# Thresholded attention and a gated feed-forward on one core: softmax turned in place in two tiles, PSUM banks of the product claimed early, operand remainders in place, and a new instruction order

## The chip, the cores and the metric

One Trainium2 chip, one of its cores. The metric is the device time of one execution in microseconds (us). Before the change it is 1448.93 us, the median of 3 runs (1448.88 to 1451.7).

## The reference, cut to what matters

Attention with 8 batches, 8 heads, 576 positions and heads of 64 in float32, then a feed-forward layer on the joined heads (512 wide, 1024 in the middle):

```python
scores = scale * np.matmul(q, k.transpose(0, 1, 3, 2))
thresh = np.max(scores, axis=-1, keepdims=True) - tau
scores = np.where(scores >= thresh, scores, -1000000000.0)
scores = scores - np.max(scores, axis=-1, keepdims=True)
attn = np.exp(scores)
attn = attn / (np.sum(attn, axis=-1, keepdims=True) + 1e-09)
x = np.matmul(attn, v)            # heads joined: batch, 576, 512
xk = mu_k * x + (1.0 - mu_k) * x_prev
xr = mu_r * x + (1.0 - mu_r) * x_prev
k = np.maximum(xk @ w_k, 0.0)
v = k * k @ w_v
r = 1.0 / (1.0 + np.exp(-(xr @ w_r)))
return r * v
```

x_prev is x moved by one position.

## The kernel before, in words

**Attention.** The unit of the attention is a *job*: one batch and one pair of heads. There are 36 of them (batch 0 is cut into two halves of 4 jobs each, batches 1 to 7 have 4 jobs each). A job has up to four units "P" of 128 query rows for both heads and a unit "T" for the last 64 rows of both heads together; a full job has the units 0, T, 1, 2, 3.

A unit goes through the engines like this. TensorE (PE) multiplies queries by keys into a PSUM tile `s` of two banks (L529, for T L503); there are two `s` tiles, so one for each head of a P unit. VectorE (DVE) takes the row maximum (L563); ScalarE (ACT) forms the threshold (L571) and the exponential into a tile `p` (L579); DVE zeroes what is below the threshold and sums (L587), then adds 1e-9 and inverts (L597, L598); GpSimd (POOL) multiplies `p` by the inverse (L612); DVE transposes 32x32 blocks of `p` into the job's tile `sq` (L630, for T L636). There are three `p` tiles and **one** `sq` tile. When all units of a job stand in `sq`, PE multiplies them by the values: 288 small matmuls (L666), here called the *product*, into four PSUM tiles `w` of one bank each; ACT copies these into `xT` and `xE` (L681, L688).

**Operands.** To keep float32 precision with the faster `fp32r` matmul, queries and keys are split: `hi` is the rounded value (ACT, L437), `lo` = `raw` - `hi` (POOL, L443). Eight DMAs of SyncE's queue (SP, L462) copy their halves into stacked tiles `st1`, `st2` (three buffers each, two used by a job); `raw` is scaled first (L419).

**Feed-forward.** When the four jobs of a batch (or half) are done, chunks of 256 positions follow, 18 in all: 16 "main" and two "end" chunks that gather the last 64 positions of four batches. A chunk has a difference (POOL, L753, tile `m`), four mixes (DVE, L762, tile `mk`), their splits (ACT L775, POOL L783), 96 matmuls for the first layer (L805), relu and square (ACT L813, L814) and split (L818, L828), 24 matmuls for the gate (L847), copy and sigmoid (ACT L851, L855), 48 matmuls for the last layer (L869), the final multiplication (DVE L875) and the store (L885). The three matmul groups take their PSUM tiles from the same tag `w` of four banks that the product uses; the product needs all four at once. The weights come as 64-bit words and are rebuilt at the start by DVE, ACT and POOL (L354 to L404).

**What sets the order.** The steps are not issued as they are written. Every step goes to `add` with an engine, a cost and a key; `Plan.order` places them one by one: of the steps that are ready it takes the one that can start first by the given costs, with ties to the lower key, and each engine then runs its instructions in that fixed order. A PSUM or SBUF buffer is given to whichever step is placed first (`loose` tags "w" and "r" in any order). Steps of the attention on PE have a key lowered by 1000; the first matmul of the product is placed only when `sq`, `v` and four `w` tiles are free for it at that moment.

Of the kernel before, what the change touches and what calls it, by code (L numbers as in the profile page):

```python
# [8 lines left out]
F32 = mybir.dt.float32  # L9
# [32 lines left out]
class Step:  # L42
    __slots__ = (
        "eng", "occ", "lat", "fn", "key", "deps", "succ", "allocs", "idx", "missing", "ready",
        "start", "end", "kb", "soft",
# [3 lines left out]
class Plan:  # L49
# [3 lines left out]
    HOP, LATE, FROM = 0.05, 0.3, 200.0  # L53
    SOFT = {"DVE": 0.3, "ACT": 0.3}
# [13 lines left out]
    def add(self, eng, occ, fn, reads=(), writes=(), key=0.0, lat=None, kb=0, wait=0.0):  # L68
        s = Step()
        s.soft = self.SOFT.get(eng, 0.0) if self.soft else 0.0  # L70
        s.eng, s.occ, s.fn, s.key, s.kb = eng, occ, fn, key, kb
# [40 lines left out]
    def order(self, loose=()):  # L112
# [27 lines left out]
        def when(s):  # L140
            t = s.ready
            hop = self.HOP
            if s.eng == "PE" and s.key < -500 and t > self.FROM:
                hop += self.LATE
# [15 lines left out]
        while len(out) < total:  # L160
# [38 lines left out]
            for j in s.succ:  # L199
# [3 lines left out]
                late = self.LATE if n.eng == "PE" and n.key < -500 and t > self.FROM else 0.0  # L203
# [14 lines left out]
def tile_threshold_attention_then_rwkv_ffn(  # L218
# [57 lines left out]
    def fixed(name, shape, dtype=F32):  # L276
# [3 lines left out]
    ident = fixed("ident", [P, P])  # L280
    add("POOL", 0.6, lambda: make_identity(nc, ident.get()), writes=[ident], key=-100)
# [9 lines left out]
        key=-100,  # L291
# [7 lines left out]
        key=-100,  # L299
# [7 lines left out]
        key=-100,  # L307
# [6 lines left out]
    for j in range(2):  # L314
        add("DVE", 0.1, lambda j=j: V.memset(xT[j].get()[:, :, 0:1], 0.0), writes=[(xT[j], "zero")], key=-99)
# [3 lines left out]
    bd = fixed("bd", [P, 2, P], FR)  # L319
    add("DVE", 0.3, lambda: V.memset(bd.get().bitcast(F32), 0.0), writes=[bd], key=-99)  # L320
# [9 lines left out]
    def weight(j, name, w, c, f, key, wait):  # L330
# [8 lines left out]
        def t():  # L339
# [9 lines left out]
            wait=wait,  # L349
# [7 lines left out]
            key=key,  # L357
# [3 lines left out]
            0.55,  # L361
            lambda: V.tensor_scalar(t(), t(), W_MIN, W_MAX, op0=ALU.max, op1=ALU.min),
            writes=box,
            key=key,
# [5 lines left out]
        def word(y):  # L370
# [4 lines left out]
            0.55,  # L375
            lambda: V.tensor_scalar(u(), u(), 0x07FFFFFF, 3, op0=ALU.bitwise_and, op1=ALU.logical_shift_left),
            writes=box,
            key=key,
# [3 lines left out]
            0.85,  # L382
# [5 lines left out]
            key=key,  # L388
# [3 lines left out]
            0.85,  # L392
# [5 lines left out]
            key=key,  # L398
        )
        add("ACT", 0.53, lambda: A.activation(piece.get()[:, 0], t(), AF.Copy), reads=box, writes=[(piece, 0)], key=key)  # L400
# [6 lines left out]
            key=key,  # L407
# [4 lines left out]
    def operands(job, key):  # L412
        b, hp = job["b"], job["hp"]
        raw = job["raw"] = sbuf("st1", [P, W], F32, 3) if job["plain"] else sbuf("raw", [P, W], F32, 1)
        add("DMA", DQ, lambda: SY.dma_start(raw.get(), qk[b, hp]), writes=[raw], key=key - PREP - 5, kb=576)
        add(
            "ACT",
            0.67,
            lambda: A.activation(raw.get()[:, 0:S], raw.get()[:, 0:S], AF.Copy, scale=small.get()[:, 2:3]),  # L419
            reads=[(small, 2)],  # L420
            writes=[raw],
            key=key - PREP,
        )
# [7 lines left out]
            kb=1152,  # L431
# [5 lines left out]
        add("ACT", 1.1, lambda: A.activation(hi.get(), raw.get(), AF.Copy), reads=[raw], writes=[hi], key=key - PREP)  # L437
        for y in range(2):
            cs = slice(0, S) if y == 0 else slice(S, W)
            add(  # L440
                "POOL",
                1.41 + 0.15 * y,
                lambda cs=cs: G.tensor_tensor(  # L443
                    lo.get()[:, cs], raw.get()[:, cs], hi.get()[:, cs].bitcast(F32), op=ALU.subtract
                ),
                reads=[raw, hi],
                writes=[(lo, y)],
                key=key - PREP,
            )
        job["st"] = [(sbuf("st1", [P, W], FR, 3), sbuf("st2", [P, S], FR, 3)) for _ in range(2)]  # L450
        for h in range(2):
            sl = slice(h * D, (h + 1) * D)
            t1, t2 = job["st"][h]

            up, dn = slice(0, D), slice(D, P)
# [526 lines left out]
```

## Time and profile before

| | |
|---|---|
| median of 3 runs | 1448.93 us |
| the profiled execution, its own time | 1451.04 us |
| its span in the profile | 1449.3 us |
| mean granted TensorE clock | 0.785 of full |
| busy: PE, DVE, ACT, POOL | 1017.6, 853.3, 643.5, 577.1 us |

The profile comes from one execution. "Busy" is time in which an engine ran at least one instruction. Since matmuls are pipelined, a busy PE is not a PE at its best rate. A row of the waits tells which engine sat idle before which line, and what ended the wait. A row of the stretches (windows) gives, for a time from A to B, its length, then for PE, PE's weight loads, DVE, ACT and POOL the busy us and the count of instructions, then the granted PE clock, the DMA share and GB/s.

### The profile page before, as it was taken

The page shows a single profiled execution, that of the slowest core. Times are in us where ns is not written, and L with a number is a line of the kernel's source. Part 1 is how long each engine was busy: PE and PEld are TensorE (multiplying, and loading weights), DVE is VectorE, ACT ScalarE, POOL GpSimd, SP SyncE. Part 2 cuts the span into 40 slices and gives each one's busy share as a digit, 9 for nine tenths or more (in the row PEclk, how much of TensorE's full clock was granted, in tenths as well). Part 3 has the DMA queues.
Part 4 walks back from the last instruction along what each step waited for, and adds up shares of the span by engine and source line. Part 5 has one row for each costly group of instructions (what it writes and reads, how often), then busy time and mean ns, then how long its engine had stood idle before and what let it go on. Part 6 is the DMA issues. An engine that isn't in the chain of part 4 may idle for free.

```text
span 1449.3 us, 34650 instructions
## 1 busy us (share of the span) xinstructions
PE 1017.6 (70%) x14608; PEld 903.6 (62%) x14608; DVE 853.3 (59%) x1657; ACT 643.5 (44%) x1447; POOL 577.1 (40%) x584
## 2 busy tenths in 40 slices
PE   3246748754995579655997568955797568955798
PEld 2236647544874478544996457854696457844687
DVE  5969648477707773477723768157753768167220
ACT  3437437243734355243743437334462437343342
POOL 3537436142713355142741337223461337222341
PEclk9558858767996579766998569975698569975799
DMA  9674644253304432254302335044422335042001
GB/s 283 193 241 124 179 140 107 73 140 115 91 27 137 114 101 56 73 140 115 91 23 69 103 100 140 23 118 121 124 57 73 102 100 136 30 116 59 2 15 30
DMA packets 41340, 147.81 MB, mean 102 GB/s; under 512 B 6880, under 2 KB 6880, under 8 KB 36576
## 3 DMA queue, kind: packets, MB, share of 16 engines
q1 hardware_dynamic: 41184, 145.59, 36.2%
q8 instruction: 116, 1.90, 0.5%
q14 instruction: 40, 0.33, 0.1%
HBM read 74.19 MB, written 9.44 MB: 58 GB/s over the span
## 4 chain that ended last, share of the span: by engine, by line
PE 60%; DVE 25%; issue 6%; DMA 5%; ACT 3%; SPq 1%; POOL 1%; DVEq 0%; POOLq 0%; ACTq 0%
PE w L666 15%; PE w L805 13%; PE w L869 13%; PE s L529 12%; DVE sq L630 7%; PE w L847 6%; DVE sm L563 6%; DVE p L587 5%; DVE mk L762 4%; DMA st<-lo 4%; ACT p L579 2%; DVE sq L636 1%; SPq L462 1%; PE s L503 1%; ACT sm L571 1%
## 5 line engine op out<-in xcount | busy, mean ns | idle before, releaser
L612 POOL TENSOR_SCALAR p<-p,sm 128x576 f32<-128x576 f32 x288 | 224.7, 792 | 537.6 <-DVE sm L598 531.8
L529 PE MATMUL s<-st 128*128 128x288 f32 x504 | 161.2, 413 | 266.8 <-DVE p L587 218.0
L666 PE MATMUL w<-sq,v 32*64 32x144 f32 (+2 forms) x10368 | 228.2, 337 | 128.7 <-issue 46.4
L666 PEld LDWEIGHTS w<-sq,v 32*64 32x64 f32 x10368 | 210.9, 170 | 149.3 <-issue 79.2
L529 PEld LDWEIGHTS s<-st 128*128 128x128 f32 x504 | 111.8, 265 | 301.5 <-issue 261.1
L630 DVE STREAM_TRANSPOSE sq<-p 128x1152 f32<-128x1152 f32 x128 | 175.4, 1370 | 181.8 <-PE w L666 172.8
L563 DVE TENSOR_REDUCE sm<-s 128x1 f32<-128x576 f32 x288 | 212.5, 750 | 89.3 <-PE s L529 79.7
L587 DVE SCALAR_TENSOR_TENSOR p<-s,sm,p 128x576 f32<-128x576 f32 x288 | 222.8, 800 | 11.0 <-ACT p L579 10.4
L805 PE MATMUL w<-xk,wk 128*128 128x256 f32 x1728 | 224.0, 288 | 4.6 <-ACT xk L775 2.4
L805 PEld LDWEIGHTS w<-xk,wk 128*128 128x128 f32 x1728 | 220.1, 196 | 6.5 <-ACT xk L775 2.8
L579 ACT ACTIVATE p<-s,sm 128x576 f32<-128x576 f32 x288 | 208.0, 725 | 0.1
L869 PE MATMUL w<-wv,k 128*128 128x512 f32 x864 | 200.6, 389 | 0.0
L571 ACT ACTIVATE sm<-sm,small 128x1 f32<-128x1 f32 x288 | 83.2, 291 | 261.1 <-DVE sm L563 257.0
L869 PEld LDWEIGHTS w<-wv,k 128*128 128x128 f32 x864 | 161.4, 188 | 32.6
L681 ACT ACTIVATE xT<-w 128x128 f32<-128x128 f32 (+1 forms) x144 | 34.4, 288 | 293.5 <-PE w L666 293.5
L875 DVE TENSOR_TENSOR sg<-w,sg 128x512 f32<-128x512 f32 x36 | 24.8, 690 | 223.5 <-PE w L869 204.1
L529 PE MATMUL s<-st,st 128*128 128x288 f32 x504 | 147.3, 385 | 0.0
L828 POOL TENSOR_TENSOR k<-r,k 128x512 fp32r<-128x512 f32 x72 | 93.5, 1300 | 94.1 <-ACT k L818 93.5
L762 DVE SCALAR_TENSOR_TENSOR mk<-m,mu_sb,xT 128x256 f32<-128x256 f32 x128 | 94.4, 778 | 42.0 <-POOL xk L783 32.0
L529 PEld LDWEIGHTS s<-st,st 128*128 128x128 f32 x504 | 116.9, 271 | 2.6 <-issue 2.5
L443 POOL TENSOR_TENSOR lo<-raw,hi 128x576 fp32r<-128x576 f32 x70 | 101.8, 1475 | 27.3 <-ACT hi L437 21.6
L783 POOL TENSOR_TENSOR xk<-mk,xk 128x512 fp32r<-128x512 f32 x72 | 92.4, 1283 | 50.1 <-ACT xk L775 49.8
(58 smaller groups left out, 934.5 us busy)
## 6 DMA issues: line engine op xcount, KB each, us to landing
v<-in_v SPq DMA_DIRECT2D x36, 1152.0 KB, 5.3
raw<-in_qk SPq DMA_DIRECT2D x35, 576.0 KB, 5.3
st<-hi SPq DMA_DIRECT2D x70, 288.0 KB, 3.1
st<-lo SPq DMA_DIRECT2D x70, 288.0 KB, 4.1
st<-hi SPq DMA_DIRECT2D x70, 144.0 KB, 3.4
st<-lo SPq DMA_DIRECT2D x70, 144.0 KB, 4.0
out<-sg SPq DMA_DIRECT2D x32, 256.0 KB, 2.0
wk<-in_w_k SPq DMA_DIRECT2D x8, 512.0 KB, 9.2
```

The costliest lines, as they stand in the source:

```text
L443: lambda cs=cs: G.tensor_tensor(lo.get()[:, cs], raw.get()[:, cs], hi.get()[:, cs].bitcast(F32), op=ALU.subtract),
L529: PE.matmul(ss[y].get()[:, z, 0:HS], l.get()[:, c * P : (c + 1) * P], r.get()[:, keys(z)], start=(j == 0), stop=(j == 1),)
L563: lambda sv=sv, col=col: V.tensor_reduce(col(0), sv(), axis=AX.XY, op=ALU.max, negate=True),
L571: lambda col=col: A.activation(col(1), col(0), AF.Identity, bias=small.get()[:, 1:2], scale=-1.0),
L579: lambda sv=sv, pv=pv, col=col: A.activation(pv(), sv(), AF.Exp, bias=col(0)),
L587: lambda sv=sv, pv=pv, col=col: V.scalar_tensor_tensor(pv(), sv(), col(1), pv(), op0=ALU.is_ge, op1=ALU.mult, accum_out=col(2)),
L612: lambda y=y: G.tensor_scalar(p.get()[:, y], p.get()[:, y], sm.get()[:, 3, y : y + 1], 0.0, op0=ALU.mult, op1=ALU.add),
L630: V.transpose(sq.get()[:, :, :, c * Q : (c + 1) * Q].rearrange("p b y i -> p y b i"), p.get().rearrange("p y (b i) -> p y b i", i=Q),)
L666: PE.matmul(os[a].get()[hs, 0:n], vt.get()[rows, j, hs], sq.get()[rows, j, h, lo:hi], start=(j == 0), stop=(j == NB - 1),)
L762: V.scalar_tensor_tensor(d.get()[:, y, o : o + n], diff.get()[:, y, o : o + n], mu_sb.get()[:, j, hc + y : hc + y + 1], prv[:, hc + y], op ...
L805: PE.matmul(h.get()[:, f], l, r, start=(ct == 0 and i == 0), stop=(ct == NCT - 1 and i == 2))
L869: PE.matmul(vps.get(), l, r, start=(ft == 0 and i == 0), stop=(ft == NFT - 1 and i == 2))
```

## The change

1. **Softmax in the job's tile.** The tiles `p` are gone. ACT's exponential writes straight into the job's `sq`, at the place where the unit's transposed blocks will stand; DVE's masking, POOL's scaling and DVE's transposition then all work in place there. `sq` has two buffers instead of one.
2. **The product's banks held ahead.** New PE steps without an instruction claim the four `w` tiles of the product (and the places in `xT`, `xE`) as soon as the last unit's inverse is computed, with the key -400; no chunk matmul can take them from then on.
3. **Remainders in place.** Queries and keys are loaded as two tiles instead of one `raw`; `lo` is written over the loaded tile. The copies into `st1`, `st2` become twelve DMAs of 144 KB instead of eight of 288 or 144 KB. For the T unit, `bd` is filled from `st1`, `st2` and its product has four steps of two matmuls instead of three.
4. **Chunk tiles.** `m` and `mk` are replaced by the two buffers of the tag `r`.
5. **The order.** Costs given to the planner are changed, a table `NUDGE` adds an offset to the key of each kind of step, and `LATE` and `SOFT` are smaller. The unused identity tile is gone.

The diff, cut to its core:

```diff
-    HOP, LATE, FROM = 0.05, 0.3, 200.0
-    SOFT = {"DVE": 0.3, "ACT": 0.3}
+    HOP, LATE, FROM, AHEAD = 0.05, 0.2, 200.0, 1000.0
+    SOFT = {"DVE": 0.15, "ACT": 0.15}
+    NUDGE = {
+        "act1": 6.0, "act10": -16.5, "act11": -27.5, "act12": -14.5, "act13": -6.0, "act14": -29.5, "act15": -3.0,
...
+        s.key = key + self.NUDGE.get(kind, 0.0)
...
-        hi, lo = job["hi"], job["lo"] = sbuf("hi", [P, W], FR), sbuf("lo", [P, W], FR)
...
+        for x, o in (("q", 0), ("k", S)):
+            raw = lo[x] = sbuf("lo" + x, [P, S], FR, LB[x])
+            top = hi[x] = sbuf("hi" + x, [P, S], FR, 1)
...
+                    raw.get(), raw.get().bitcast(F32), top.get().bitcast(F32), op=ALU.subtract
...
-            prods = [(0, hi), (0, lo), (1, hi)]
...
+            for h in range(2):
+                for v_ in range(2):
...
-        p = unit["p"] = sbuf("p", [P, 2, S], F32, PB)
+        sm = unit["sm"] = sbuf("sm", [P, 4, 2], F32, 4)
+        if job["sq"] is None:
+            job["sq"] = sbuf("sq", [P, NB, 2, NX], F32, 2)
...
+        def part(y):
+            if unit["kind"] == "P":
+                return sq.get()[:, :, y, c * Q : (c + 1) * Q]
+            return sq.get()[:, :, :, P:NX].rearrange("p b y i -> p (b y) i")
...
-            V.transpose(
-                sq.get()[:, :, :, c * Q : (c + 1) * Q].rearrange("p b y i -> p y b i"),
-                p.get().rearrange("p y (b i) -> p y b i", i=Q),
-            )
+            t = sq.get()[:, :, :, c * Q : (c + 1) * Q].rearrange("p b y i -> p (b y) i")
+            V.transpose(t, t)
...
+        last = job["units"][-1]
+        for o in os:
+            add("PE", 0.0, lambda: None, reads=[(last["sm"], (RES, 1))], writes=[o, *main, *tail], key=-400.0, lat=0.0, kind="pe4")
...
-            diff = sbuf("m", [P, 2, CH], F32, 1)
+            diff = sbuf("r", [P, 2, CH], F32, 2)
...
-                d = sbuf("mk", [P, 2, CH], F32, 1)
+                d = sbuf("r", [P, 2, CH], F32, 2)
```

How the order moves is shown at two places of the steady part of the program. First PE, around a job's product. Before, at the end of a batch (L869 is the last layer of a chunk, L666 the product; the last number in a tile's name tells one use from another):

```order
L869 MATMUL w_3_6187<-wv50_0_1485,k2_0_6058 128x512 x3
L869 MATMUL w_3_6187<-wv60_0_1684,k2_0_6058 128x512 x3
L869 MATMUL w_3_6187<-wv70_0_1689,k2_0_6058 128x512 x3
L666 MATMUL w_0_6216<-sq_0_5549,v_0_5547 64x144
L666 MATMUL w_1_6218<-sq_0_5549,v_0_5547 64x144
L666 MATMUL w_2_6220<-sq_0_5549,v_0_5547 64x144
L666 MATMUL w_3_6222<-sq_0_5549,v_0_5547 64x144
```

The changed kernel, one job's product (L843 is the first layer, L559 a score, L705 the product):

```order
L526 MATMUL s_1_7520<-st1_2_7118,bd_74 128x288 x4
L526 MATMUL s_1_7520<-st1_0_7394,bd_74 128x288 x4
L843 MATMUL w_2_7498<-xk_0_7214,wk31_0_623 128x256 x3
L843 MATMUL w_2_7498<-xk_0_7214,wk01_0_585 128x256 x3
L843 MATMUL w_2_7498<-xk_0_7214,wk11_0_601 128x256 x3
L843 MATMUL w_2_7498<-xk_0_7214,wk21_0_611 128x256 x3
L559 MATMUL s_0_7564<-st1_2_7118 128x288 x2
L559 MATMUL s_0_7564<-st1_2_7118,st2_1_7127 128x288 x2
L705 MATMUL w_3_7580<-sq_0_7057,v_0_7315 64x144
L705 MATMUL w_0_7582<-sq_0_7057,v_0_7315 64x144
```

Before, the product of a batch's last job stood behind the whole of two chunks, with no score matmul among the last 45 of L869, 96 of L805, 24 of L847 and 48 of L869. Now the product stands inside a chunk (its first layer goes on behind it) and scores of the next job stand just ahead of it. In the whole steady part of the new order one chunk lies spread over two jobs, and no more than 33 chunk matmuls stand between two scores. At the end of the program, after the last product, come 24 matmuls of L907 and then four whole chunks (96 of L843, 24 of L885, 48 of L907 each), where before there were three.

Second DVE, at the same two places. Before (L875 is the last step of a chunk, L630 and L636 transpose, L587 masks):

```order
L875 TENSOR_TENSOR sg_0_5899<-w_3_5972,sg_0_5899 128x512
L875 TENSOR_TENSOR sg_0_6149<-w_2_6160,sg_0_6149 128x512
L875 TENSOR_TENSOR sg_0_6149<-w_3_6187,sg_0_6149 128x512
L630 STREAM_TRANSPOSE sq_0_6366<-p_2_5768 128x2x18x32
L636 STREAM_TRANSPOSE sq_0_6366<-p_0_5847 128x36x16
L630 STREAM_TRANSPOSE sq_0_6366<-p_1_5888 128x2x18x32
L587 SCALAR_TENSOR_TENSOR p_2_6377,sm_0_5927<-s_0_5913,sm_0_5927,p_2_6377 128x576
```

And now (L605 maximum, L629 masks, L671 and L675 transpose, L639 and L640 invert):

```order
L605 TENSOR_REDUCE sm_1_7538<-s_1_7520 128x1
L629 SCALAR_TENSOR_TENSOR sq_1_7487,sm_2_7465<-s_0_7513,sm_2_7465,sq_1_7487 128x18x32
L671 STREAM_TRANSPOSE sq_0_7057<-sq_0_7057 128x36x32
L639 TENSOR_SCALAR sm_2_7465<-sm_2_7465 128x2
L640 RECIPROCAL sm_2_7465<-sm_2_7465 128x2
L629 SCALAR_TENSOR_TENSOR sq_1_7487,sm_1_7538<-s_1_7520,sm_1_7538,sq_1_7487 128x36x16
L605 TENSOR_REDUCE sm_3_7658<-s_0_7564 128x1
L639 TENSOR_SCALAR sm_1_7538<-sm_1_7538 128x1
L640 RECIPROCAL sm_1_7538<-sm_1_7538 128x1
L629 SCALAR_TENSOR_TENSOR sq_1_7487,sm_3_7658<-s_0_7564,sm_3_7658,sq_1_7487 128x18x32
L671 STREAM_TRANSPOSE sq_1_7487<-sq_1_7487 128x36x32
```

Before, the three transpositions into the next job's `sq` stood behind the chunks' last steps and needed the one `sq` that the product above (of `sq_0_5549`) still had to read. Now, behind the last transposition of a job (`sq_0_7057`), DVE has masks, a maximum and a transposition of the next job in the other tile (`sq_1_7487`) before it needs anything that PE makes after the product.

More of the change, by code (lines that the diff above doesn't have):

```diff
@@ L5 @@
 from concourse import mybir
-from concourse.masks import make_identity
 from concourse._compat import with_exitstack
@@ L348, in weight @@
             kb=512,
-            wait=wait,
+            wait=wait, kind="dma2",
         )
@@ L413, in operands, with scaled @@
         b, hp = job["b"], job["hp"]
[L414 to L422, printed above, removed]
-        )
+        def scaled(t):
+            add(
+                "ACT",
+                0.67,
+                lambda: A.activation(t()[:, 0:S], t()[:, 0:S], AF.Copy, scale=small.get()[:, 2:3]),
+                reads=[(small, 2)],
+                writes=[raw],
+                key=key - PREP, kind="act3",
+            )
+        if job["plain"]:
+            raw = job["raw"] = sbuf("st1", [P, W], F32, 3)
+            add("DMA", DQ, lambda: SY.dma_start(raw.get(), qk[b, hp]), writes=[raw], key=key - PREP - 5, kb=576, kind="dma3")
+            scaled(raw.get)
         vt = job["v"] = sbuf("v", [P, NB, P], F32, VB)
@@ L435, in operands @@
             return
-        hi, lo = job["hi"], job["lo"] = sbuf("hi", [P, W], FR), sbuf("lo", [P, W], FR)
-        add("ACT", 1.1, lambda: A.activation(hi.get(), raw.get(), AF.Copy), reads=[raw], writes=[hi], key=key - PREP)
-        for y in range(2):
-            cs = slice(0, S) if y == 0 else slice(S, W)
+        hi, lo = job["hi"], job["lo"] = {}, {}
+        st = job["st"] = [(sbuf("st1", [P, W], FR, 3), sbuf("st2", [P, S], FR, 3)) for _ in range(2)]
+        up, dn = slice(0, D), slice(D, P)
@@ new lines, in operands @@
+                lambda raw=raw, top=top: G.tensor_tensor(
+                    raw.get(), raw.get().bitcast(F32), top.get().bitcast(F32), op=ALU.subtract
+                ),
+                reads=[top],
+                writes=[raw],
+                key=key - PREP, kind="pool2",
+            )
+            for h in range(2):
+                sl = slice(h * D, (h + 1) * D)
+                moves = [(st[h][0], up, top), (st[h][0], dn, raw)]
+                if x == "q":
+                    moves += [(st[h][1], dn, top), (st[h][1], up, raw)]
+                for dst, rows, src in moves:
+                    fn = (lambda dst=dst, rows=rows, src=src, sl=sl, o=o: SY.dma_start(
+                        dst.get()[rows, o : o + S].bitcast(F32), src.get()[sl].bitcast(F32)
+                    ))
+                    add("DMA", DQ, fn, reads=[src], writes=[(dst, (rows.start, x))], key=key - PREP, kb=144, kind="dma6")
@@ L519, in both @@
                         )
-            add("PE", 3.0, both, reads=[raw], writes=list(ss.values()), key=key - 1000, lat=3.25)
+            add("PE", 3.0, both, reads=[raw], writes=list(ss.values()), key=key - 1000, lat=3.25, kind="pe2")
             return
@@ L769, in scale @@
                             )
-                add("DVE", 0.9 if nseg == 1 else 1.6, scale, reads=[diff, mu_sb, *sr], writes=[d], key=key)
+                add("DVE", 0.8 if nseg == 1 else 1.6, scale, reads=[diff, mu_sb, *sr], writes=[d], key=key, kind="dve14")
                 add(
```

227 lines of the change are left out of this document (114 added, 113 removed), and 6 rows, old and new, of the table NUDGE.

## The prediction

> **What bounds the kernel now.** I read the page first, then the stretches, the waits, the chain, and the timeline around one product. The page's first part gives no engine as the bound:
>
> ```profile
> PE 1017.6 (70%) x14608; PEld 903.6 (62%) x14608; DVE 853.3 (59%) x1657; ACT 643.5 (44%) x1447; POOL 577.1 (40%) x584
> ```
>
> No engine is busy over 70%, so the question is who waits for whom. The stretches tell it (from:to, length, busy us of PE, weight loads, DVE, ACT, POOL, granted clock):
>
> ```profile
> 0.00:210.00 210.00, 104.94 (x2624) 91.18 (x2624) 154.01 (x267) 97.30 (x214) 99.45 (x91) 0.73 0.67 195
> 453.00:473.00 20.00, 9.88 (x153) 8.83 (x138) 15.70 (x30) 9.81 (x27) 8.04 (x8) 0.67 0.63 171
> 518.00:550.00 32.00, 27.10 (x179) 25.53 (x177) 29.35 (x60) 25.48 (x59) 24.19 (x24) 0.89 0.58 153
> 534.00:550.00 16.00, 16.00 (x110) 14.86 (x108) 14.10 (x33) 14.89 (x31) 13.91 (x14) 1.00 0.45 104
> 561.00:589.00 28.00, 28.00 (x173) 24.86 (x173) 1.45 (x3) 9.71 (x15) 6.42 (x5) 1.00 0.06 20
> 943.00:1105.00 162.00, 119.00 (x1646) 106.59 (x1638) 96.27 (x188) 73.38 (x168) 63.72 (x65) 0.78 0.35 95
> ```
>
> 943:1105 is one whole batch: 4 jobs, 2 chunks, 162 us or 40.5 us a job, in which DVE works 96.27 us and PE 119.00. In 561:589, a whole chunk, PE works alone (DVE 1.45 of 28 us); in 453:473, attention alone, PE works half the time at 0.67 of its clock. Only in 518:550 do chunk and attention run side by side, and there DVE is busy 0.92 and PE 0.85 of the time. The two engines take turns, and the sum of the turns is the time. The waits of DVE show where its turns end (us in all, times, longest):
>
> ```profile
> DVE sg L875 <- PE w L869: 204.1, 24, 21.7
> DVE sq L630 <- PE w L666: 172.8, 30, 7.7
> DVE sm L563 <- PE s L529: 79.7, 150, 10.1
> ```
>
> 204.1 us DVE stands before a chunk's last step, which its fixed order puts ahead of the next softmax work; 172.8 us it stands before a transposition into `sq` until the product has read `sq`. The chain around one such place (start, us), then PE's and DVE's timeline there:
>
> ```profile
> 561.13 11.38 PE w L805 x96
> 572.51 5.50 PE w L847 x24
> 578.01 10.89 PE w L869 x48
> 588.93 0.70 DVE sg L875
> ```
> ```profile
> 588.82 0.47 PE L666 MATMUL w<-sq,v 32*64 32x144 f32 x6
> 589.68 4.21 PE L666 MATMUL w<-sq,v 32*64 32x144 f32 x254 [0.39 <-DVE sg L875]
> 595.03 0.74 PE L666 MATMUL w<-sq,v 32*64 32x144 f32 x28 [1.14 <-issue]
> ```
> ```profile
> 595.92 1.38 DVE L630 STREAM_TRANSPOSE sq<-p 128x1152 f32<-128x1152 f32 x1 [6.30 <-PE w L666]
> ```
>
> A chunk costs PE 11.38 + 5.50 + 10.89 = 27.77 us. The product waits behind it, since the chunk had the `w` tiles, then takes 595.77 - 588.82 = 6.95 us, and DVE waits 6.30 us of these.
>
> **The change part by part.**
>
> *Two `sq` tiles, banks held ahead, new order.* They remove together the two waits above: the product no longer stands behind two chunks (PE order), and DVE has the next job's work in another tile during the product (DVE order). What is late next is then either engine's own work. I count it for the 28 full jobs of batches 1 to 7, between which the new order spreads 13 chunks. On a PE at full clock a pair of score matmuls takes 0.26 us, read from starts 0.26 apart:
>
> ```profile
> 517.99 0.42 PE L503 MATMUL s<-lo,bd 128*128 128x288 f32 x2
> 518.25 0.43 PE L503 MATMUL s<-hi,bd 128*128 128x288 f32 x2
> ```
>
> so 0.13 each. A job has 32 of them and 8 for T (6 before; the 2 more cost 0.26 us a job): 5.2 us. With 6.95 for the product, PE needs 28 x 12.15 = 340 us, and 13 x 27.77 = 361 for the chunks, less 5.4 (half of 10.89) for the 24 matmuls that stand behind the last product: 696 us. DVE: 853.3 in all, less 154 for the start (row 0:210), less what belongs to the four chunks at the end. That is, from the rows below, for two main chunks 2 x (8 x 0.778 + 2 x 0.690) = 15.2 and for two end chunks 2 x (32 x 0.308 + 1.4) = 22.5, in all 38. There remain 661 us.
>
> ```profile
> L762 DVE SCALAR_TENSOR_TENSOR mk<-m,mu_sb,xT 128x256 f32<-128x256 f32 x128 | 94.4, 778 | 42.0 <-POOL xk L783 32.0 <-POOL m L753 10.0
> L762 DVE SCALAR_TENSOR_TENSOR mk<-m,mu_sb,xE 128x64 f32<-128x64 f32 x64 | 15.3, 308 | 33.7 <-POOL xk L783 33.7
> L875 DVE TENSOR_TENSOR sg<-w,sg 128x512 f32<-128x512 f32 x36 | 24.8, 690 | 223.5 <-PE w L869 204.1
> ```
>
> So PE has 696 us and DVE 661 us of work in the same stretch, and the bound is whichever is more, at the share that a fixed order can reach. In 518:550 the busier engine reached 0.92. I take that: 696 / 0.92 = 757 us, or 27.0 us a job. The row 534:550 (PE 1.00, DVE 0.88) would be the good end, 0.97 as an estimate; 0.85, between these and the attention alone (453:473: DVE 0.785), the bad one: 718 to 819.
>
> *The claim of the banks* adds no instruction, but from the last inverse until the product's copies are out no new chunk matmul group can start; queued behind is the rest of the chunk, and who waits is PE. The price is the way from inverse to product, two scalings and a transposition, less the chunk and score matmuls that the order keeps there (15 and 4 in the place shown, 15 x 0.12 + 4 x 0.13 = 2.3 us from 11.38 / 96):
>
> ```profile
> L612 POOL TENSOR_SCALAR p<-p,sm 128x576 f32<-128x576 f32 x288 | 224.7, 792 | 537.6 <-DVE sm L598 531.8 <-DVE xT L362 3.0 <-DVE sm L597 2.8
> L630 DVE STREAM_TRANSPOSE sq<-p 128x1152 f32<-128x1152 f32 x128 | 175.4, 1370 | 181.8 <-PE w L666 172.8 <-POOL p L612 8.8
> ```
>
> 2 x 0.79 + 1.37 = 2.95, so under 1 us a job, inside the 0.92.
>
> *Softmax in place.* The same counts of instructions of the same sizes. L630 already writes in runs of 32; now L579, L587 and L612 do too. No row shows these so; the nearest are the two transpositions, which write runs of 32 and, below, of 16.
>
> ```profile
> L636 DVE STREAM_TRANSPOSE sq<-p 128x576 f32<-128x576 f32 x32 | 24.0, 751 | 0.0
> ```
>
> For 1152 elements that is 1.37 against 1.50 us, so a run's length moves an instruction by 0.13 us. I take nothing, with 0.13 either way as bounds: 14 masks and transpositions a job, 28 x 14 x 0.13 = 51 us either way on DVE, of which the 35 us that it has less than PE hide most. POOL has 63.72 / 4 = 16 us of work a job, and could lose 11 us before it counts.
>
> *Remainders in place.* The rows of the split, of one copy's issue (ns: least, median, most) and of a table load:
>
> ```profile
> L437 ACT ACTIVATE hi<-raw 128x1152 fp32r<-128x1152 f32 x35 | 40.7, 1164 | 7.9 <-PE s L503 4.2 <-issue 3.2
> L462 SPq DMA_DIRECT2D st<-lo x140: 461/595/1662, 11.9 to 1309.2; - x140
> L855 ACT ACT_TABLE_LOAD x9 | 11.5, 1283 | 0.2
> ```
>
> `hi` becomes two instructions of half the size, some 0.58 us each as an estimate, and up to 0.2 us more of ACT a job. SP issues 14 operand DMAs a job instead of 9; with 0.6 us each that is 8.4 us of 27.
>
> *Table loads.* The new order has 28 on ACT, before 18: 10 x 1.28 = 13 us more, on an engine with 73.38 / 4 = 18 us of work a job. Hidden.
>
> *Start and end.* Until the 8th half-job DVE works 154.01 of 210 us; without the wait for the product I take 0.80 (0.73 now, 0.90 at best): 192 us (171 to 211). The end is the last product 6.95, the rest of a chunk 5.4, four chunks 111.1, and the last step and store:
>
> ```profile
> 1433.76 10.89 PE w L869 x48
> 1444.68 0.69 DVE sg L875
> ```
>
> 1449.3 - 1444.65 = 4.65. Together 128 us; one chunk more than now (28 us) is spent there, and is in the sum.
>
> **Sum**: 192 + 757 + 128 = 1077 us of span. The profiled execution took 1451.04 for a span of 1449.3 (+1.7), the median of the runs is 2.1 below it, so span and median are the same within 0.4. Forecast **1077 us**, faster by 372.
>
> **The rivals.**
>
> *POOL in DVE's way.* An L762 takes 0.48 us in the median and up to 1.65:
>
> ```profile
> L762 DVE SCALAR_TENSOR_TENSOR mk<-m,mu_sb,xT x128: 465/484/1646, 67.3 to 1384.8; 128x256 f32<-128x256 f32 x128
> L597 DVE TENSOR_SCALAR sm<-sm x160: 119/168/1241, 13.5 to 1343.2; 128x2 f32<-128x2 f32 x128, 128x1 f32<-128x1 f32 x32
> ```
>
> With a mean of 0.778 that is 0.29 us of delay on each, and POOL's share goes from 63.72 / 162 = 0.39 to 16 / 27 = 0.59. If the delay grows as the share does, it costs 13 x 8 x 0.15 = 16 us, inside the range. If it triples, 13 x 8 x 0.6 = 62, and as much as 20 on L597: DVE 743 / 0.92 = 808, in all 1128 us. [...] Chance 0.09.
>
> *The clock.* Scores in the attention alone, after a gap of 2.34 us:
>
> ```profile
> 466.15 0.82 PE L529 MATMUL s<-st 128*128 128x288 f32 x2 [2.34 <-DVE p L587]
> 466.77 0.68 PE L529 MATMUL s<-st,st 128*128 128x288 f32 x2
> 467.25 0.68 PE L529 MATMUL s<-st 128*128 128x288 f32 x2
> ```
>
> If PE keeps the 0.89 of 518:550 instead of 1.00, 696 / 0.89 / 0.92 = 850, in all 1170 us. For it: in attention alone the clock is 0.67. Against: 534:550 with 1.00. [...] The trace is less kind: after the gap of 2.34 us the pairs of score matmuls start 0.48 apart, near half rate. Chance 0.07.
>
> *The second tile changes nothing*: DVE waits on for the product, at 172.8 / 36 = 4.8 us a job: 28 x 4.8 = 134, in all 1211 us. The DVE order shown speaks against it. Chance 0.05.
>
> *A faster product.* 254 of its 288 matmuls took 4.21 us; without the gap a product is 4.8 us, PE has 636, DVE bounds with 661 / 0.95 = 696, in all 171 + 696 + 126 = 993 us. The gap of 1.14 "issue" stands against it. Chance 0.05.
>
> *The other side: the operands are late.* All of a job's operands go through single tiles now, so load, scaling, split, remainder and copies can become one chain between two jobs. From the rows it is 5.3 + 0.78 + 0.58 + 1.48 + 6 x 0.60 + 4.1 = 15.8 us:
>
> ```profile
> raw<-in_qk SPq DMA_DIRECT2D x35, 576.0 KB, 5.3
> st<-lo SPq DMA_DIRECT2D x70, 288.0 KB, 4.1
> L419 ACT ACTIVATE raw<-raw,small 128x576 f32<-128x576 f32 x35 | 27.3, 780 | 9.8 <-DMA raw<-in_qk 9.8
> L443 POOL TENSOR_TENSOR lo<-raw,hi 128x576 fp32r<-128x576 f32 x70 | 101.8, 1475 | 27.3 <-ACT hi L437 21.6 <-issue 4.1 <-DMA st<-lo 0.5
> ```
>
> Wholly exposed: 1077 + 28 x 15.8 = 1519 us, slower. It decides from 372 / 28 = 13.3 us a job. Against it: the third `st1` buffer still lets one head's copies start early. Chance 0.03.
>
> **How the numbers follow.** Forecast 0.70 (its own range 1017 to 1158: 171 + 718 + 128 to 211 + 819 + 128); POOL 0.09; clock 0.07; faster product 0.05; second tile without effect 0.05; operands late 0.03; no change 0.01. The range 1010 to 1180, a little beyond these and the clock's 1170, holds the first three, 0.86. A measurement here tells about 0.2% (3 us) from no change. Faster: 0.96, same 0.01, slower 0.03.
>
> **What would show it.** Right: DVE's waits for L666 before transpositions gone; a batch every 108 us with DVE and PE both near 0.9 and the clock near 1.00; four chunks alone at the end, 111 us. Wrong: a period above 125 us for a batch; DVE's maxima (L605) waiting for scores by more than 3 us a job; PE waiting for `st`; the product still near 7 us with a clock below 0.9.

## The result, and the profile after

| | before | after |
|---|---|---|
| median | 1450.04 us, 4 runs (1448.88 to 1451.7) | 1133.57 us, 4 runs (1132.94 to 1137.41) |
| ratio, 95% interval | | 0.7822 (0.7802 to 0.7842) |
| span of the profiled execution | 1449.3 us | 1131.3 us |

The forecast was 1077 us with a range of 1010 to 1180. The time fell by 316 us where 372 were forecast. The first part of the page of after shows what the turns of PE and DVE have become:

```profile
PE 922.5 (82%) x14672; PEld 822.8 (73%) x14672; DVE 841.9 (74%) x1657; ACT 649.1 (57%) x1492; POOL 573.1 (51%) x582
```

Nearly the same instructions as before, in a shorter span. DVE has 11 us less work than before. PE is busy for 95 us less with 64 matmuls more, at a mean granted clock of 0.921 where it was 0.785; its share of the span went from 70% to 82%. The stretches of after are cut as the prediction's sum is: start, middle, end. Behind them stand two batches of the middle, and then the first two pieces of the middle, which are slower:

```profile
0.00:211.70 211.70, 112.45 (x2653) 98.69 (x2654) 159.60 (x284) 100.79 (x233) 103.35 (x94) 0.74 0.66 197
211.70:993.50 781.80, 683.56 (x11039) 612.30 (x11039) 659.34 (x1310) 499.39 (x1177) 421.95 (x443) 0.96 0.48 132
993.50:1131.30 137.80, 126.54 (x984) 111.76 (x984) 22.98 (x64) 48.94 (x83) 47.82 (x45) 0.97 0.06 20
401.00:625.00 224.00, 201.76 (x3296) 180.94 (x3296) 191.06 (x377) 149.33 (x349) 127.18 (x131) 0.99 0.50 138
212.00:300.00 88.00, 68.41 (x1160) 60.66 (x1160) 71.65 (x143) 52.33 (x132) 41.00 (x44) 0.90 0.51 141
300.00:400.00 100.00, 84.55 (x1253) 76.22 (x1254) 84.32 (x166) 60.14 (x144) 51.51 (x56) 0.86 0.48 131
```

Two batches take 224 us, 112 each, where one took 162. Chunk and attention now run side by side all the time: PE is busy 0.90 and DVE 0.85 of it. The clock is 0.99 there, and lowest in the first 190 us of the middle (the last two rows). The waits of DVE in the whole of after (times of all waits, how many, the longest):

```profile
DVE sm L605 <- PE s L559: 102.3, 113, 7.2
DVE r L800 <- POOL r L791: 57.9, 8, 15.2
DVE sg L913 <- issue: 39.0, 4, 22.5
DVE sq L629 <- ACT sq L621: 23.3, 39, 2.5
```

The waits for the last layer in front of the chunk's last step (204.1 us) and for the product in front of a transposition (172.8) are gone. The rows of L800 and L913 lie nearly all in the end (52.6 of 57.9 us, and all 39.0), where DVE has nothing else to do. What is left of weight is the maximum's wait for scores. The timelines of PE and of DVE around one product of the middle show what it is:

```profile
625.42 2.66 PE L705 MATMUL w<-sq,v 32*64 32x144 f32 x146 [0.73 <-DVE sm L639]
629.41 2.27 PE L705 MATMUL w<-sq,v 32*64 32x144 f32 x128 [1.34 <-issue]
632.88 0.50 PE L705 MATMUL w<-sq,v 32*64 32x144 f32 x14 [1.20 <-issue]
```
```profile
634.15 1.42 DVE L605 TENSOR_REDUCE sm<-s 128x1 f32<-128x576 f32 x2 [2.69 <-PE s L559]
```

The product still takes 632.88 + 0.50 - 625.42 = 7.96 us here, in three pieces with pauses of over a microsecond, for which the profile names no releaser ("issue"; the last section has what goes with them). DVE no longer waits for the product itself. It works on in the other tile, then stands 2.69 us until the scores that PE runs behind the product are there. The largest waits of PE in the middle, 211.7 to 993.5 us, are these pauses and the wait of a score for its PSUM tile, which the mask must have read first:

```profile
PE w L705 <- issue: 43.0, 32, 2.3
PE s L559 <- DVE sq L629: 32.5, 26, 2.5
```

### The profile page after: what moved, and what is told of

It reads as the page before. It is cut to its first block, busy times and chain, and to the rows that moved or that the text cites. A ratio compares the mean times of both kernels' runs of the same rounds, so it can differ in the third digit from the quotient of the medians.

```text
span 1131.3 us, 35156 instructions
## 1 busy us (share of the span) xinstructions
PE 922.5 (82%) x14672; PEld 822.8 (73%) x14672; DVE 841.9 (74%) x1657; ACT 649.1 (57%) x1492; POOL 573.1 (51%) x582
## 4 chain that ended last, share of the span: by engine, by line
PE 49%; DVE 24%; issue 12%; ACT 9%; POOL 5%; DMA 1%; SPq 0%; POOLq 0%; ACTq 0%; DVEq 0%
PE w L705 16%; PE s L559 9%; PE w L843 9%; PE w L907 8%; DVE sq L671 6%; PE w L885 6%; DVE sm L605 6%; DVE sq L629 6%; DVE r L800 3%; ACT sq L621 3%; POOL sq L654 2%; PE s L526 1%; ACT k L856 1%; ACT sm L613 1%; DVE sg L913 1%
## 5 line engine op out<-in xcount | busy, mean ns | idle before, releaser
L654 POOL TENSOR_SCALAR sq<-sq,sm 128x576 f32<-128x576 f32 x288 | 227.3, 802 | 235.5 <-DVE sm L640 228.0
L605 DVE TENSOR_REDUCE sm<-s 128x1 f32<-128x576 f32 x288 | 212.5, 751 | 117.1 <-PE s L559 102.3
L705 PE MATMUL w<-sq,v 32*64 32x144 f32 (+2 forms) x10368 | 193.3, 297 | 121.3 <-issue 98.2
L705 PEld LDWEIGHTS w<-sq,v 32*64 32x64 f32 x10368 | 172.3, 146 | 142.3 <-issue 114.2
L629 DVE SCALAR_TENSOR_TENSOR sq<-s,sm,sq 128x576 f32<-128x576 f32 x288 | 226.2, 803 | 24.7 <-ACT sq L621 23.3
L843 PE MATMUL w<-xk,wk 128*128 128x256 f32 x1728 | 226.9, 289 | 8.1 <-ACT xk L813 4.0
L843 PEld LDWEIGHTS w<-xk,wk 128*128 128x128 f32 x1728 | 221.0, 195 | 11.3 <-POOL xk L821 5.0
L907 PE MATMUL w<-wv,k 128*128 128x512 f32 x864 | 214.8, 396 | 0.4 <-ACT xE L726 0.4
L621 ACT ACTIVATE sq<-s,sm 128x576 f32<-128x576 f32 x288 | 208.9, 726 | 0.2
L671 DVE STREAM_TRANSPOSE sq<-sq 128x1152 f32<-128x1152 f32 x128 | 175.4, 1371 | 16.1 <-POOL sq L654 15.9
L907 PEld LDWEIGHTS w<-wv,k 128*128 128x128 f32 x864 | 161.3, 191 | 31.2 <-ACT xE L726 0.7
L559 PE MATMUL s<-st 128*128 128x288 f32 x504 | 125.4, 333 | 56.9 <-DVE sq L629 41.6
L559 PEld LDWEIGHTS s<-st 128*128 128x128 f32 x504 | 89.5, 205 | 84.0 <-issue 58.8
L821 POOL TENSOR_TENSOR xk<-r,xk 128x512 fp32r<-128x512 f32 x72 | 92.4, 1283 | 101.8 <-ACT xk L813 100.7
L559 PE MATMUL s<-st,st 128*128 128x288 f32 x504 | 117.0, 315 | 0.6 <-issue 0.6
L800 DVE SCALAR_TENSOR_TENSOR r<-r,mu_sb,xT 128x256 f32<-128x256 f32 x128 | 74.3, 620 | 52.5 <-POOL r L791 44.1
L885 PE MATMUL w<-wr,xk 128*128 128x512 f32 x432 | 107.8, 391 | 0.0
L719 ACT ACTIVATE xT<-w 128x128 f32<-128x128 f32 (+1 forms) x144 | 34.5, 288 | 99.7 <-PE w L705 99.7
L559 PEld LDWEIGHTS s<-st,st 128*128 128x128 f32 x504 | 89.2, 207 | 1.1 <-issue 1.1
L885 PEld LDWEIGHTS w<-wr,xk 128*128 128x128 f32 x432 | 78.1, 188 | 13.2
```

Of the source, the lines that this page charges most:

```text
L559: PE.matmul(ss[y].get()[:, z, 0:HS], l.get()[:, c * P : (c + 1) * P], r.get()[:, keys(z)], start=(j == 0), stop=(j == 1),)
L605: lambda sv=sv, col=col: V.tensor_reduce(col(0), sv(), axis=AX.XY, op=ALU.max, negate=True),
L621: lambda st=st, pv=pv, col=col: A.activation(pv(), st(), AF.Exp, bias=col(0)),
L629: lambda st=st, pv=pv, col=col: V.scalar_tensor_tensor(pv(), st(), col(1), pv(), op0=ALU.is_ge, op1=ALU.mult, accum_out=col(2)),
L654: lambda y=y: G.tensor_scalar(part(y), part(y), sm.get()[:, 3, y : y + 1], 0.0, op0=ALU.mult, op1=ALU.add),
L671: V.transpose(t, t)
```

## The experiments

Two questions were open. First, which part of the change brought the time: the prediction's theory is that claim, second tile and order do it together; the rival is that one part carries it nearly alone. Second, what holds a batch at 112 us where 108 were forecast: the theory is PE's own work with its pauses; the rivals are DVE's work, and the place of the product ahead of the scores that DVE waits for, which another order would mend. A ratio is to runs of the kernel before on the same chip, and a difference of two ratios is uncertain by about 0.0035, or 5 us. The letters of the theories are those of the expectations; what they call e5 is experiment 7 here, and e9 is experiment 9.

**1. After without the claim.** The product's banks go to whoever is placed first, as before the change.

```diff
-        last = job["units"][-1]
-        for o in os:
-            add("PE", 0.0, lambda: None, reads=[(last["sm"], (RES, 1))], writes=[o, *main, *tail], key=-400.0, lat=0.0, kind="pe4")
...
-            add("PE", occ, mm, reads=[vt, sq], writes=os, ...)
+            add("PE", occ, mm, reads=[vt, sq], writes=[*os, *([*main, *tail] if k == 0 else [])], ...)
```

> The changed kernel without the early claim of the four product banks; two sq tiles, work in place and the key table stay, and the planner orders the rest anew. Its order puts 48 matmuls of a chunk's last layer just ahead of every second product again. Theory A (the gain is the end of turn-taking, and the claim is what lets the chunk be spread): about 1250 us, at least 1180; DVE waits for the product or for scores behind it by 80 us or more in addition. Theory B (the key table makes the order, the claim is a detail): under 1155. Theory C (the second sq tile alone is the gain): under 1155, with DVE's waits before transpositions still gone.

Measured: 1301.19 us, ratio 0.8954 (0.8938 to 0.8969). So everything else together takes 10.5% off the time of before, and the claim on top of it another 11.3 points. Theories B and C fell. Theory A's least of 1180 held, but not the place of its waits: the maximum's wait for scores hardly grew, and DVE waits for exponentials and for the last layer instead, 23.3 and 10.4 us in after. (ACT, which makes the exponentials, waits 190.4 us for the product before its copies, 99.7 in after.)

```profile
DVE sq L629 <- ACT sq L621: 96.9, 40, 8.9
...
DVE sg L910 <- PE w L904: 52.1, 18, 4.9
```

**2. After with one `sq` tile.**

```diff
-            job["sq"] = sbuf("sq", [P, NB, 2, NX], F32, 2)
+            job["sq"] = sbuf("sq", [P, NB, 2, NX], F32, 1)
```

> The changed kernel with one sq tile instead of two; claim and table stay. Theory A: DVE and ACT cannot begin the next job in the tile before the product has read it, 7 us of product less the 2.7 us that DVE already waits there, about 4 to 5 us for each of 28 jobs: 1134 + 120 = about 1255, at least 1200. Theory C (second tile is everything): 1400 or more. Theory B: under 1160.

Measured: 1326.62 us, ratio 0.912 (0.9075 to 0.9166). The loss is larger than theory A's, and theories B and C fell. The first of DVE's waits in this kernel says how:

```profile
DVE sq L629 <- ACT sq L621: 232.2, 44, 10.3
```

DVE waits for exponentials, up to 10.3 us each: with the tiles `p` gone and a single `sq`, ACT has no place to write an exponential of the next job until the product has read the tile. In-place work seems to need the second tile more than the old way did: experiment 3, with one `sq` and the three `p` tiles, is 136 us faster, though its order differs too.

**3. Before with the claim alone.** Three lines are added to the kernel before, and the product itself no longer claims its places in `xT` and `xE`; the kernel keeps its three `p` tiles, one `sq`, old operands and old costs.

```diff
-        sm = sbuf("sm", [P, 4, 2], F32, 4)
+        sm = unit["sm"] = sbuf("sm", [P, 4, 2], F32, 4)
...
+        last = job["units"][-1]
+        for o in os:
+            add("PE", 0.0, lambda: None, reads=[(last["sm"], (3, 1))], writes=[o, *main, *tail], key=-400.0, lat=0.0)
...
-            free = [*main, *tail] if k == 0 else []
-            add("PE", occ, mm, reads=[vt, sq], writes=[*os, *free], key=key - 1000, lat=occ + 0.25)
+            add("PE", occ, mm, reads=[vt, sq], writes=os, key=key - 1000, lat=occ + 0.25)
```

> The kernel before with nothing but the early claim of the product's banks (its three p tiles, one sq, its keys and costs stay). Its order now spreads a chunk over two jobs. Theory A: most of the solid chunk time in which DVE stands is filled, the wait before the transpositions stays: about 1260 us. Theory C: about 1450, no change. Theory B: above 1400.

Measured: 1190.81 us, ratio 0.8197 (0.8174 to 0.822). The claim alone brings 18.0% where the whole change brings 21.8%, 70 us more than theory A expected; theories B and C fell. The waits of DVE:

```profile
DVE sq L630 <- PE w L669: 111.3, 29, 8.0
...
DVE sg L877 <- PE w L871: 29.7, 4, 21.7
```

The wait of the chunk's last step (L877) falls from 204.1 to 29.7 us, four times in all. The wait of the transposition for the product (L669 here) falls only from 172.8 to 111.3; these waits are gone in after.

**4. After without the table of offsets** (`NUDGE` empty; the planner's new costs stay).

```diff
-    NUDGE = {
-        "act1": 6.0, "act10": -16.5, "act11": -27.5, "act12": -14.5, "act13": -6.0, "act14": -29.5, "act15": -3.0,
...
+    NUDGE = {}
```

> The changed kernel with the table of key offsets emptied; costs, claim, tiles as changed. Theory A: the chunk is spread all the same, 1150 to 1175 us. Theory B: the table is the gain, 1250 or more.

Measured: 1170.88 us, ratio 0.8039 (0.801 to 0.8068). The table is worth 0.8039 - 0.7822 = 0.0217 of the time of before, 31 us, as theory A expected.

**5. DVE's load.** Line 639 is left out of after, so the 1e-9 is not added to the sums; the order is the same otherwise.

```diff
-            V.tensor_scalar(sm.get()[:, 2, ysl], sm.get()[:, 2, ysl], 1e-9, None, op0=ALU.add)
```

> The changed kernel in the same order, without the addition of 1e-9 to the sum (L639), 160 instructions of DVE with 51 us in all; it leaves that addition out. If DVE bounds: about 1134 - 45 = 1090. If PE alone bounds: 1125 or more. If both bind each other: about 1110.

Measured: 1135.14 us, ratio 0.781 (0.7785 to 0.7834), which can't be told from after's. The first row is the line that was taken out, in after; the second is the wait for scores in this kernel:

```profile
L639 DVE TENSOR_SCALAR sm<-sm 128x2 f32<-128x2 f32 (+1 forms) x160 | 51.0, 319 | 0.9
```
```profile
DVE sm L605 <- PE s L559: 149.2, 139, 7.2
```

51 us of DVE's work went, and its wait for scores grew by 149.2 - 102.3 = 47. Taking work from DVE alone gains nothing here.

**6. PE's load.** The product leaves out 8 of the 18 key blocks, so it has 160 matmuls instead of 288.

```diff
-                for j in range(k * NB // KC, (k + 1) * NB // KC):
+                for j in (j for j in range(k * NB // KC, (k + 1) * NB // KC) if j % 2 == 0 or j == NB - 1):
```

> The changed kernel in the same order with 160 of the 288 matmuls of each product (leaves out 8 of 18 blocks of keys). The product takes 7.1 us now; with 320 instructions instead of 576 and at most one gap, 3.5 to 4. If PE's time is fully on the path: 36 x 3.3 = 119 us less, 1015. If DVE bounds: DVE's wait behind the product goes, 2 us a job, 1060 to 1080, and then DVE's busy share in the middle is above 0.92.

Measured: 1051.29 us, ratio 0.7234 (0.7211 to 0.7257), that is 0.0588 or 85 us off after. The group of the product's matmuls in after and in this kernel (busy, mean ns of one | idle before, and its reasons), then DVE's wait for scores in this kernel:

```profile
L705 PE MATMUL w<-sq,v 32*64 32x144 f32 (+2 forms) x10368 | 193.3, 297 | 121.3 <-issue 98.2 <-DVE sq L671 14.4 <-DVE sm L639 6.0
```
```profile
L705 PE MATMUL w<-sq,v 32*64 32x144 f32 (+2 forms) x5760 | 111.9, 302 | 75.4 <-issue 52.5 <-DVE sq L671 12.9 <-DVE sm L639 7.3
```
```profile
DVE sm L605 <- PE s L559: 34.0, 61, 3.7
```

PE is busy 193.3 - 111.9 = 81 us less in the product. Of the idle "issue", 54.2 us in after and 40.0 here lie in the start, most of it in waits of 8 to 9 us ahead of a product and not inside one; from the middle on the pauses fall from 44.0 to 12.5. Together that is 113 us less of PE's time, and 85 us come off the whole, three quarters. So PE's product is on the path, but not alone: the time lies between the 1015 of PE alone and the 1060 to 1080 of DVE, whose busy share between 212 and 911 us is 0.89 now.

**7. The product in two halves.** If DVE waits for scores that stand behind the product, the second half of the product can stand behind the next two units' scores. In the order that the planner gave, the second step of each product, and what hangs on it, is moved behind up to four score steps.

```diff
     plan.order(loose=("w", "r"))
+    halves = [i for i in plan.out if plan.steps[i].kind == "pe5"][1::2]
+    for h in halves:
...
+        for j in pe[:4]:
+            if plan.steps[plan.out[j]].kind not in ("pe1", "pe3"):
+                break
+            last = j
...
+        plan.out[at : last + 1] = stay + moved
     plan.issue()
```

> The changed kernel, its planned order altered at one place per job: the second half of the product (144 matmuls) goes behind the next two scores (8 score matmuls), so DVE need not wait for the whole product. DVE waits for scores 86 us in the 28 full jobs of the changed kernel, 2.69 us behind the product looked at, where the scores could have started in the middle. Theory D (DVE and PE bind each other, the head of PE's queue is the wait): 28 x 1 to 2.5 us less, about 1085 us, and some of the start too. Theory E (PE alone bounds, its work is the same): 1125 to 1140.

Measured: 1147.55 us, ratio 0.7889 (0.7866 to 0.7913), 0.0067 above after, and a little above the 1140 of theory E; theory D fell. The waits of DVE in this kernel:

```profile
DVE sq L629 <- ACT sq L621: 85.7, 50, 5.7
...
DVE sm L605 <- PE s L559: 44.4, 79, 3.7
```

The wait for scores did fall, from 102.3 to 44.4. In its place DVE waits for exponentials, 85.7 after 23.3. ACT's waits tell why, first in after, then here:

```profile
ACT xT L719 <- PE w L705: 99.7, 37, 8.1
```
```profile
ACT xT L719 <- PE w L705: 127.4, 38, 8.7
```

ACT's fixed order has the copies of the product ahead of the next exponentials, so it stands there until the later half is done. Experiment 9 moves the copies.

**8. The same without line 639**: experiments 5 and 7 together.

> Both together: the product in two halves around the scores, and no addition of 1e-9 (left out). Theory D: 1050 to 1070 us. Theory E: 1120 or more.

Measured: 1136.63 us, ratio 0.7826 (0.7802 to 0.785), as theory E expected: 11 of the 51 us count here, while none counted in after.

**9. Halves, and ACT's copies late.** As 7, and the copies are moved behind the two exponentials of those scores.

```diff
+        exps = [j for j in range(at + 1, len(plan.out)) if plan.steps[plan.out[j]].kind == "act7" and ...]
+        last_mm, last = last, max(exps)
...
-        plan.out[at : last + 1] = stay + moved
+        plan.out[at : last + 1] = stay[: mm + 1] + [h] + stay[mm + 1 :] + moved[1:]
```

> As e5 (product cut in two around the next two scores), but the copies of the product on ScalarE now stand behind the two exponentials of these scores in its order; in e5 they stood ahead of them and DVE's waits for exponentials rose from 23 to 86 us. Theory D (DVE and PE bind each other, and e5 only moved the wait to ScalarE's queue): 1075 to 1115 us. Theory E (PE alone bounds): within 1 per cent of 1134.

Measured: 1165.77 us, ratio 0.8031 (0.8011 to 0.805). Theory D fell, and theory E's 1 per cent was missed too: it is 2.7 per cent above after. DVE's waits and then PE's, where the wait went:

```profile
DVE sm L605 <- PE s L559: 117.9, 76, 5.4
...
DVE sq L629 <- ACT sq L621: 32.1, 40, 5.2
```
```profile
PE w L907 <- ACT xE L726: 16.4, 14, 2.8
PE w L843 <- ACT xE L726: 13.7, 12, 2.0
```

The wait for exponentials is small again (32.1), but the product's banks come free later: PE stands 16.4 + 13.7 us for the copies before chunk matmuls, where after has 0.4 us of the first wait and none of the second. DVE waits 117.9 us for scores again; that this follows from PE's wait for the copies is likely but not shown.

**10. The same without line 639**: experiments 5 and 9 together.

> e9 without the addition of 1e-9 (left out). If DVE is on the path again once the scores come early: 15 to 40 us below e9. If PE alone bounds: as e9.

Measured: 1157.64 us, ratio 0.7979 (0.7952 to 0.8007). Of DVE's 51 us 8 count, between the two expectations.

**11. Wider product matmuls.** Each of the 288 matmuls of a product moves 288 columns instead of 144, and only half of what it computes is of use; the count of instructions is the same. It was run once, so its time has no interval.

```diff
-                                os[a].get()[hs, 0:n],
+                                os[a].get()[hs, 0 : 2 * n].rearrange("p (y i) -> p y i", y=2),
...
-                                sq.get()[rows, j, h, lo:hi],
+                                sq.get()[rows, j, :, lo:hi],
```

> The changed kernel with twice the columns in each matmul of the product (288 for 144: both heads' probabilities against one head's values, the second half is written beside the result and not used); the instructions are as many as before, but each takes the array twice as long. Theory F (PE runs out of instructions: the gaps inside a product are a whole number of 256 instructions apart): the pairs start 35 ns apart, the issue gaps before L705 fall from 98 us to under 30, a product takes 10 us or more, and the whole 1190 to 1240. Theory G (the gaps belong to the banks or the data of the product): the gaps stay near 98 us or grow.

Measured: 1193.51 us. PE's timeline at one product of the middle, and PE's waits between 230 and 950 us, here and then in after:

```profile
629.91 8.99 PE L705 MATMUL w<-sq,v 32*64 32x288 f32 x288
```
```profile
PE s L559 <- DVE sq L629: 31.5, 24, 3.5
PE w L705 <- DVE sm L639: 5.1, 7, 0.8
PE w L705 <- DVE sq L671: 3.8, 2, 3.1
```
```profile
PE w L705 <- issue: 42.0, 31, 2.3
```

A matmul now takes 8.99 / 288 = 31 ns, where it was 2.27 / 128 = 18 in the piece at 629.41 us of after, and the pauses are gone: 42.0 us in 31 pauses before, no row of "issue" in front of the product now. Over the whole program that row falls from 98.2 to 29.3 us; theory F's figures for that row and for the whole hold, though a matmul takes less than its 35 ns and a product less than its 10 us. So the pauses were gone when the matmuls followed each other 31 ns apart and not 18, with 288 of them in a product as before.

## Why the prediction was right, and where its sizes were off

**The mechanism held.** Two engines took turns, the two waits that made them were removed, and what came after is an interleaved order in which PE is the busier engine. Of the signs named ahead, the waits for the product before transpositions are gone, the clock is near 1.00 (0.96 in the middle, 0.99 in two batches of it), and the period is 112 us, between the 108 forecast and the 125 named as wrong. The product at 7.1 us (below) is the sign against, though at a clock of 0.96. The four chunks at the end take 121 us, not 111. And one sign of being wrong came, by a little: the maximum's waits for scores, those of the T units among them, are 80.7 + 5.4 us in the middle, 3.1 us a job where 3 was the border.

```profile
DVE sm L605 <- PE s L559: 80.7, 94, 4.0
...
DVE sm L605 <- PE s L526: 5.4, 14, 0.9
```

**What brought the time.** The prediction priced the claim, the second tile and the order together. Experiment 3 shows that the claim alone is worth 262 us on the kernel before, and experiment 1 that it is worth 0.8954 - 0.7822, 164 us, on top of the rest. The parts don't add up: the claim without the second tile and the new order leaves 111.3 us of waits for the product, and the rest without the claim leaves chunks in the product's way. In the whole change the second tile is worth 0.912 - 0.7822, 188 us, and the table 31. What the second tile brings without the claim on the kernel before, and what the operands, the chunk's tiles and the costs bring by themselves, no run tells.

**Start: 192 forecast, 211.7 measured, 210 before.** Here the step "without the wait for the product I take 0.80" failed; DVE is busy 159.60 / 211.70 = 0.75. (The new order also puts 5.6 us more of DVE's work into this stretch; at 0.80 it would take 199.5.) The rows of DVE's waits in the start, before and then after:

```profile
DVE sm L563 <- PE s L529: 13.7, 6, 8.0
DVE sq L630 <- PE w L666: 13.1, 3, 7.2
```
```profile
DVE sm L605 <- PE s L559: 21.6, 19, 7.2
```

Only 13.1 us of the wait for the product stood here, a number that the prediction didn't look up, and most of it came back as a wait for scores that stand behind the product. The clock in the start is 0.74, before 0.73.

**Middle: 757 forecast, 781.8 measured.** DVE's work was forecast at 661 us and is 659.34. PE's was forecast at 696, which counts 28 products with their pauses; one of them is the last product, which the end counts too, so 689 is the number to compare, and 1069 would have been the forecast. Measured are 683.56 us busy and 43.0 us of pauses in the product, 726.6. Most of the 38 us between is the clock: 689 less 27 x 1.14 of pauses is 658, and at 0.96 that is 686 (an estimate; busy were 683.56). The rest is the pauses: 43.0 instead of 31. Of the 55 us in which PE neither worked nor paused in a product, 32.5 are the wait for a mask. The share, on the other hand, came out as chosen: 726.6 / 781.8 = 0.93 against 0.92. There is luck in that, since 0.92 was DVE's busy share in a stretch of 32 us, and 0.93 is PE's with its pauses counted as work. Experiments 5 and 6 show that "whichever is more" was PE: 51 us less on DVE changed nothing, 113 less on PE took 85 off.

The step that failed here is that the sum took PE at full clock throughout. The granted clock falls to half eleven times in the middle, six of them up to 344 us. PE's timeline at three of these falls, then two of the stretches there:

```profile
282.63 0.82 PE L559 MATMUL s<-st 128*128 128x288 f32 x2 [3.49 <-DMA out<-sg]
...
288.93 3.94 PE L705 MATMUL w<-sq,v 32*64 32x144 f32 x144 [3.09 <-DVE sq L671]
...
299.88 0.65 PE L559 MATMUL s<-st 128*128 128x288 f32 x2 [1.72 <-DVE sq L629]
```
```profile
295.00:297.00 2.00, 1.96 (x85) 1.53 (x68) 2.00 (x3) 1.37 (x8) 0.00 (x0) 1.00 0.04 8
300.00:320.00 20.00, 14.33 (x258) 12.10 (x262) 16.78 (x34) 7.96 (x19) 9.38 (x11) 0.57 0.53 133
```

Ahead of two of the eleven falls stand gaps of 3.49 and 3.09 us. From 295 to 297 us the clock is full again, and the long slow stretch from 300 us on, at 0.57, stands behind a gap of only 1.72 us; the longest gaps at the other eight falls are 1.77 to 2.47 us, and four of these are pauses of the product. The last section has a gap of 2.29 us that no fall followed, and what goes with a fall.

**End: 128 forecast, 137.8 measured.** The four chunks don't follow each other without a break. PE's timeline at their ends:

```profile
1063.19 1.33 PE L843 MATMUL w<-xk,wk 128*128 128x256 f32 x7
1065.48 10.89 PE L843 MATMUL w<-xk,wk 128*128 128x256 f32 x89 [0.96 <-POOL xk L821]
...
1092.56 0.89 PE L843 MATMUL w<-xk,wk 128*128 128x256 f32 x6
1095.73 0.58 PE L843 MATMUL w<-xk,wk 128*128 128x256 f32 x1 [2.28 <-ACT xk L813]
1097.07 13.16 PE L843 MATMUL w<-xk,wk 128*128 128x256 f32 x89 [0.76 <-POOL xk L821]
```

A chunk starts with 6 or 7 matmuls, then waits for the split of its mix. The last one has 2.28 + 0.76 us of idle time, and then 89 matmuls take 13.16 us where 10.89 is usual. From 1063.19 to 1092.56 a chunk takes 29.37 us instead of the 27.77 that the prediction took from a chunk whose mix stood ready.

**The small terms.** Softmax in place and its runs of 32 cost nothing: the exponential takes 726 ns (before 725), the mask 803 (800), the scaling 802 (792), the transposition 1371 (1370). The smaller and more frequent copies land sooner (2.5 to 3.0 us from issue to landing, before 3.1 to 4.1 for both sizes).

**The rivals.** POOL in DVE's way fell: the mixes got faster, the addition of 1e-9 slower, in sum no loss. The group of the mixes in after, and of the addition in before (L597):

```profile
L800 DVE SCALAR_TENSOR_TENSOR r<-r,mu_sb,xT 128x256 f32<-128x256 f32 x128 | 74.3, 620 | 52.5 <-POOL r L791 44.1 <-POOL xk L821 8.5
```
```profile
L597 DVE TENSOR_SCALAR sm<-sm 128x2 f32<-128x2 f32 (+1 forms) x160 | 35.3, 220 | 1.9
```

778 to 620 ns is 20 us less on DVE; the addition went from 35.3 to the 51.0 of experiment 5's first row, 16 more. That POOL's delay falls on these two lines alone, as the rival's 743 us has it, no run shows; in after the mean maximum takes 751 ns (before 750) and the mean mask 803 (800). The clock held at 0.89 fell as a steady state, with a part of it true in the first two batches. The product was not faster: (148.56 busy + 43.0) / 27 = 7.1 us each. The late operands fell: in the middle no wait of PE for a copy into `st` stands among its rows. That the second tile changes nothing fell by name, since DVE's transpositions don't wait; but a part of its price, 3.1 of 4.8 us a job, is paid in front of the scores instead.

**What stays open.** None of the rearrangements (7 to 10) beats after. Whether a planner that knew of PE's pauses and of ACT's place between product and exponential could reach the forecast's 108 us a batch was not tried.

## What to carry to other kernels

When two engines take turns, look first for the resource that lets one group of work lock out another: here three lines that reserve four banks ahead of time brought, alone, 262 us, where the whole change brought 316. The parts lean on one another, though: taken out of the whole, the claim and the second tile each cost more than half of it (164 and 188 us). Test which engine bounds by taking work from each in turn: less work on DVE only lengthened its waits, less on PE shortened the kernel until DVE was as busy. And look up each wait in the stretch where you count on its removal; a total over the program says nothing of the start.

## What the runs showed of the hardware

**The pauses.** The prediction counted one pause of 1.14 us in each product; there are 32 in the middle's 27 products, and they cost 43.0 us, 1.6 us a product. Worked out from the start times in the trace of after, with PE's matmuls, weight loads and waits for semaphores counted together, the 31 distances between them are 256 to 1537 instructions, each within one of a multiple of 256. The page's row of the instruction queue in after (packets, MB, share):

```profile
q8 instruction: 116, 1.90, 0.7%
```

1.90 MB in 116 packets is 16.4 KB a packet; how many instructions that is, no run shows.

The trace of after keeps the start and the length of each of these packets. All 32 pauses of the middle end 1.23 to 1.57 us after the end of a packet; there are 89 packets in these 782 us, so that by chance about one pause in 25 would. The closest two packets start 3.30 us apart. 256 instructions of a product, 128 matmuls with their weight loads, take 2.27 us in the piece at 629.41 us; in experiment 11 they take 128 x 31 ns = 4.0 us, and the pauses are gone. That PE waits for its instructions in a pause is the author's estimate from these times; the profile names no releaser there.

**The clock.** In the trace of after each of the 40 records of the granted clock is either full or half, and each starts a multiple of 3.41 us after the first. What goes with a fall there is how busy PE was in the 3.41 us just ended, worked out from the start and the (modelled) end of each matmul. Of 269 such windows at full clock, 20 were followed by half clock, and in these PE was busy 0.48 of the time or less; in the other 249 it was busy 0.50 or more. The same working on the trace of before gives 231 windows, 33 of them followed by half clock, with 0.49 or less in these and 0.48 or more in the other 198. In after no fall followed the gap of 2.29 us ahead of 266.86 us, and one followed the gap of 1.72 us. So in these two traces a fall went with PE's busy share, not with the length of one gap; what sets the clock they don't show.
